# Choosing PSUM accumulation banks by the planner's count of when they come free, instead of from one ring

## The chip, the core and the metric

The kernel runs on one core of a Trainium2 chip. The time is device microseconds for one launch, the median of several launches. The engines are called as the profile calls them: PE (TensorE, matmul), DVE (VectorE), ACT (ScalarE), POOL (GpSimd) and SP (SyncE, which issues most of the DMAs here). PE writes its results into PSUM, which the kernel uses as eight banks of 128 x 512 float32. Only DVE and ACT read the banks in this kernel, and a bank can take a new result when its last reader is through.

## What is computed

The output mixes two branches over the same input `x` (2048 tokens of 576 channels) with a gate for each token:

```python
g = sigmoid((x * gate_w).sum(-1, keepdims=True))
a = ssm_branch(x, A_re, A_im, B_re, B_im, C_re, C_im, log_dt, Dskip)
b = expert_branch(x, w_q, k1, k2, u, v)
return g * a + (1 - g) * b
```

The first branch builds, for each channel, a kernel of 2048 taps from 128 complex exponentials, convolves `x` with it by FFT, and adds `x * Dskip`. The second has 32 heads. Each head forms a query of 2 x 128 for a token, scores each half against 64 keys, takes the best two of each half, combines them to four candidates and keeps two. That makes 64 experts of 4096 for each token, with softmax weights `g`:

```python
act = gelu(einsum("nd,nhkd->nhk", x, u[top_e]))
out = einsum("nhk,nhk,nhkd->nd", g, act, v[top_e])
```

## The kernel before

The kernel doesn't gather experts. It multiplies `x` with all of `u`, selects by one-hot matrices, and multiplies the selected weights with all of `v`. Its matmuls, with the names that they bear in the profile:

- `a` (128 tiles of 14 matmuls of 128 x 512, named `a{c}_{tb}_{j}`): `x` times `u` for one eighth `c` of the experts, one quarter `tb` of the tokens and one 128-row piece `j`. `act_post` copies each tile out of its bank as `go` (ACT or DVE) and stores it in `g_d`.
- `s` (128 tiles of 14 matmuls, `s{c}_{t}`): the scores of token tile `t` (of 16) in column group `c` (of 8). `scores_top` reads the bank sixteen times on DVE: eight MAX8, then eight FIND_INDEX8.
- `wb`, `wn`, `sq`, `x`, `kn`: folding of query weights with keys (giving `whl`), and norms for scaling.
- `kP`, `wbp`, `kb`: phases and taps of the convolution kernel, 36 channel groups `c` (`k_front`, `k_gen`, `k_store`); `gn` is a norm for them. ACT, POOL and DVE work on each group between its `kP` and its `kb`.
- `u` (`u1_{p}`, 16 steps that need four banks at once), `k` (`k1_{w}`), `pr`/`pi`, `pv`: FFT of the input, FFT of the taps, products of the spectra and the step back (`u_stage1`, `k_stage1`, `products`). `k_stage1` starts when all `kb` are stored.
- `tr`: transposes of the indices, after the gating of all column groups.
- `S{t}_{q}_{hb}`: for token tile `t` and quarter `q`, two banks of 16 short matmuls of one-hot matrices `A` and `Bg`, which DVE builds. DVE multiplies them into `gl`, and `split` makes `wh` of `gl` by an ACT and a DVE pass. Token tiles come in the order 0, 15, 1, 14, 2, ...
- `o` (16 token tiles of two banks, 3,072 matmuls of 128 x 288): `wh` times `vhl`, which `v_work` makes of `v` in eight pieces `vhl0` to `vhl7`, each by ACT and by DVE or POOL passes. `y` (8 steps that need four banks at once) is the last step of the inverse FFT, added into `ya`.

**What sets the order.** The Python program carries its own planner. Each piece of work is a generator, `clock` is the planner's time on PE, and each engine has a count of when it will be free (`Engine.free`). `rdy` holds when a tile will be ready. A generator yields until its inputs are ready and then writes its instructions at the end of the engines' queues. The main loop (lines 1719 to 1757) chooses between an `s` tile and an `a` tile. It holds `s` back when DVE's count is far ahead of PE (`lag`), and `pump` lets the other generators in between groups of three matmuls. On the chip each engine runs its queue strictly in that order, so an instruction that waits holds up all behind it.

**Banks.** A quota by tag says how many banks the three kinds of users may hold: `sc` (the `s`, `a` and `o` tiles), `kb` (convolution work) and later `wb` (the same after line 921). Each tag has a list of times at which its own places come free (`slots`). `need(tag, n)` waits until `n` places of that tag are free by the planner's clock, `take` removes the earliest, and `free(tag, outs)` adds one with the time at which the reader's output will be ready. Which of the eight banks a tile gets is not in that count: the pool is asked for a buffer of one shared tag.

```python
288  quota(sc=4, wb=0, kb=4, hw=1, slot=9, go=3, m8=2, raw=1, ko=1)
290  def bank(tag, name):
291      take(tag, name)
292      t = ps.tile([128, 512], F32, tag="ps", name=name, bufs=8)
1696 bank_free = lambda: slots["sc"] and min(slots["sc"]) <= clock[0]
```

A matmul into a bank whose former readers have not finished waits on PE, whatever the quota said.

Of the kernel before, what the change touches and what calls it, by code (L numbers as in the profile page):

```python
# [138 lines left out]
def body(ctx: ExitStack, tc: tile.TileContext, xT, au, par, logdt, dskip, gatew, wq, kT, uT, vv,  # L139
# [5 lines left out]
    clock = [0.0]  # L145
# [296 lines left out]
    def squares(a, r, sq, dst):  # L442

        acc = newcol(), newcol()
        S.activation(sq[:, 0:4, :], a, AF.Square, accum_out=sc[:, acc[0]])
        S.activation(sq[:, 4, :], r, AF.Square, accum_out=sc[:, acc[1]])
        yield from ready(sq)
        tag = side()
        yield from need(tag)
        p = bank(tag, "sq")  # L450
        mm(p[:, 0:2], onesb, short(acc[0].start, 2), True, True, 0.05)
        yield from ready(p)
        V.tensor_reduce(out=dst, in_=p[:, 0:2], axis=AX, op=OP.add)
        free(tag, dst)
# [5 lines left out]
    def x_norm(tb, sq):  # L460

        yield from need("kb")
        p = bank("kb", f"x{tb}")
        if tb == 0:
            for k in range(8):
                mm(p, onesb, sq[:, k % 4, :], True, True)
            while not marks["s"]:
                yield 0.1
        for k in range(5):
            mm(p, onesb, sq[:, k, :], k == 0, k == 4)  # L470
        normed.append(tb)
# [4 lines left out]
        free("kb", nx)  # L476
# [23 lines left out]
    def scale_first(a, r, sq, keep=None):  # L500
# [16 lines left out]
        free("kb", out[0])  # L517
# [80 lines left out]
    def w_half(c, h, w):  # L598
# [22 lines left out]
        free(tag, s)  # L621
# [19 lines left out]
    def w_tail(c, k, pb, hl, rem, o, count, s, tag):  # L641
        yield from ready(pb, s)
        if k < 4:
            yield from split(hl[:, 0, k:k + 2, o], hl[:, 1, k:k + 2, o], pb.rearrange("p (k n) -> p k n", k=2), s)
            free(tag, hl)
        else:
# [8 lines left out]
            free(tag, rem)  # L655
# [29 lines left out]
    def k_params():  # L685
# [82 lines left out]
        for h in range(2):  # L768
# [5 lines left out]
            free("kb", sc[:, b[h]])  # L774
# [10 lines left out]
    def k_factors(g):  # L785
# [8 lines left out]
        free("kb", t)  # L794
# [6 lines left out]
    def k_front(c):  # L801
# [18 lines left out]
        def reduce(z, p):  # L820
# [9 lines left out]
            free("kb", CS)  # L830
# [82 lines left out]
    def k_store(c, kb):  # L913
# [9 lines left out]
        free("kb", ko)  # L923
# [28 lines left out]
    def scores_top(c, t, pb):  # L952
# [14 lines left out]
        free("sc", i8)  # L967
# [76 lines left out]
    def turned(t, p):  # L1044
# [3 lines left out]
        free("wb", idxT)  # L1048
# [14 lines left out]
    def u_stage1():  # L1063
# [18 lines left out]
        def tail(p, tag, pbs):  # L1082
            for g in range(2):
                o = us[:, 2 + g, :]
                for hh in range(2):
# [4 lines left out]
                    free(tag, ov)  # L1090
# [43 lines left out]
    def k_stage1(ksb, fk, tabs):  # L1134
        enter, leave, count = ring(3)

        def tail(w, o, pbs):
            yield from ready(*pbs)
            for hh in range(2):
                copy(o[:, 288 * hh:288 * hh + 288], pbs[hh][:, :288])  # L1140
                free("wb", o)
# [22 lines left out]
    def products(ff):  # L1164
# [21 lines left out]
        def tail(g, pbs, v):  # L1186

            t = ff.tile([128, 2, 2, PW], F32, tag="tt", name=f"tt{g}", bufs=2)
            for n, p in enumerate(pbs):
                yield from ready(p)  # L1190
                copy(t[:, n].rearrange("p u q -> p (u q)"), p)
                free("wb", t)
# [10 lines left out]
        def store(g, pvs):  # L1203
# [4 lines left out]
            for n in range(2):  # L1208
                free("wb", vos[k])
# [167 lines left out]
    def act_post(c, tb, j, pb):  # L1377
# [8 lines left out]
        free("sc", go)  # L1386
# [9 lines left out]
    def v_norm():  # L1396
# [12 lines left out]
        for b in range(48):  # L1409
# [22 lines left out]
            free(tag, sv[0])  # L1432
# [62 lines left out]
    def prep(t):  # L1495
# [14 lines left out]
        for q in range(4):  # L1510
# [13 lines left out]
            for hb, pS in enumerate(pbs):  # L1524
# [5 lines left out]
                free("wb", *gl)  # L1530
# [27 lines left out]
    def y_part():  # L1558
# [16 lines left out]
        for p in range(NT // 2):  # L1575
# [16 lines left out]
            for n, a in enumerate(ya):  # L1592
                yield from ready(a, *pbs[2 * n:2 * n + 2])
                for hh in range(2):
                    ah = a[:, 288 * hh:288 * hh + 288]
                    V.scalar_tensor_tensor(ah, pbs[2 * n + hh][:, :288], iuk, ah, op0=OP.mult, op1=OP.add)
                    free("wb", a)
# [12 lines left out]
    def half_rows(t, a, po, hh):  # L1610
        cs = slice(288 * hh, 288 * hh + 288)
        V.scalar_tensor_tensor(a[:, cs], po[hh][:, :288], om[:, t:t + 1], a[:, cs], op0=OP.mult, op1=OP.add)
        free("sc", a)
# [44 lines left out]
    def k_split():  # L1658
# [10 lines left out]
        free("kb", kk)  # L1669
# [26 lines left out]
    bank_free = lambda: slots["sc"] and min(slots["sc"]) <= clock[0]  # L1696
# [143 lines left out]
```

## Time and profile before

| | us |
|---|---|
| median of 3 runs (lowest, highest) | 1455.22 (1452.94, 1456.87) |
| the profiled execution's own time | 1458.63 |
| span of its trace, first to last instruction | 1456.8 |
| mean granted TensorE clock | 0.998 |
| PE busy | 1430.8 (98%) |
| DVE busy | 1221.0 (84%) |
| ACT busy | 776.0 (53%) |
| POOL busy | 521.4 (36%) |

The span is the time between the first and the last instruction; the run's own time has 1.8 us around it. Busy time is the share in which an engine had an instruction in work. In the list of waits, a row names the waiting engine and its tile, the engine and tile that ended the wait, and then the sum in us, the number of such waits and the longest. In the timeline a row has start, duration, engine, line, operation, output and input tiles and count, and in square brackets the idle time before it with what ended that. PEclk is the granted TensorE clock as a share of full speed.

### The profile page before, as it was taken

The page shows a single profiled execution, that of the slowest core. Times are in us where ns is not written, and L with a number is a line of the kernel's source. Part 1 is how long each engine was busy: PE and PEld are TensorE (multiplying, and loading weights), DVE is VectorE, ACT ScalarE, POOL GpSimd, SP SyncE. Part 2 cuts the span into 40 slices and gives each one's busy share as a digit, 9 for nine tenths or more (in the row PEclk, how much of TensorE's full clock was granted, in tenths as well). Part 3 has the DMA queues.
Part 4 walks back from the last instruction along what each step waited for, and adds up shares of the span by engine and source line. Part 5 has one row for each costly group of instructions (what it writes and reads, how often), then busy time and mean ns, then how long its engine had stood idle before and what let it go on. Part 6 is the DMA issues. An engine that isn't in the chain of part 4 may idle for free.

```text
span 1456.8 us, 36814 instructions
## 1 busy us (share of the span) xinstructions
PE 1430.8 (98%) x14103; PEld 853.9 (59%) x14105; DVE 1221.0 (84%) x4569; ACT 776.0 (53%) x1304; POOL 521.4 (36%) x510
## 2 busy tenths in 40 slices
PE   7999999999999999999999999999899999999998
PEld 3445445555454445455555444447687887888787
DVE  6898889889877996885989898689998988998860
ACT  6346776796685776834556564576333224323310
POOL 0335357536446446210237999623000100110100
PEclk9999999999999999999999999999999999999999
DMA  8235223442434432269486776787343432342400
GB/s 306 77 112 172 88 80 109 126 138 72 129 106 124 116 104 92 62 211 292 157 304 216 266 250 214 255 265 228 130 122 110 140 120 98 125 148 67 157 9 17
DMA packets 134352, 215.44 MB, mean 148 GB/s; under 512 B 10912, under 2 KB 79904, under 8 KB 127776
## 3 DMA queue, kind: packets, MB, share of 16 engines
q1 hardware_dynamic: 134080, 213.01, 45.3%
q8 instruction: 111, 1.82, 0.5%
q14 instruction: 65, 0.53, 0.1%
q10 hardware_dynamic: 96, 0.07, 0.0%
HBM read 141.74 MB, written 71.30 MB: 146 GB/s over the span
## 4 chain that ended last, share of the span: by engine, by line
PE 85%; DVE 5%; DMA 2%; ACT 1%; issue 0%; POOL 0%; SPq 0%; DVEq 0%; POOLq 0%
PE o L214 25%; PE s L214 22%; PE a L214 22%; PE S L214 4%; PE kb L214 2%; PE wb L214 2%; PE pr L214 2%; DMA vn<-in_au_dram 1%; PE y L214 1%; PE kP L214 1%; PE k L214 1%; DVE i L134 1%; PE pv L214 1%; PE u L214 1%; DVE vhl L134 1%; DVE m L134 1%
## 5 line engine op out<-in xcount | busy, mean ns | idle before, releaser
L214 PE MATMUL o<-vhl,wh 128*128 128x288 f16 x3072 | 389.2, 287 | 0.0
L214 PE MATMUL s<-whl,xb 128*128 128x512 f16 x1536 | 365.0, 379 | 0.0
L214 PE MATMUL a<-xb,uhl 128*128 128x512 f16 x1536 | 359.5, 379 | 0.2 <-DVE go L134 0.2
L214 PEld LDWEIGHTS <-wh 128*128 128x128 f16 x3072 | 296.8, 98 | 77.5 <-issue 3.7
L214 PEld LDWEIGHTS <-xb 128*128 128x128 f16 x1792 | 170.6, 98 | 208.5 <-issue 14.3
L214 PEld LDWEIGHTS <-uhl 128*128 128x128 f16 x1536 | 147.1, 98 | 176.3 <-issue 3.2
L134 DVE FIND_INDEX8 i<-m,s 128x8 uint32<-128x64 f32 x1024 | 206.9, 226 | 0.0
L134 ACT ACTIVATE wh<-gl,s_wg 128x1024 f16<-128x1024 f32 x64 | 69.0, 1137 | 203.6 <-DVE gl L134 203.6
L134 DVE MAX8 m<-s 128x8 f32<-128x64 f32 x1024 | 146.4, 217 | 27.1 <-PE s L214 26.6
L134 POOL TENSOR_TENSOR CS<-CS,ex 128x512 f32<-128x512 f32 x72 | 97.9, 1389 | 147.6 <-DVE ex L134 146.2
L134 POOL TENSOR_TENSOR ya<-ya,db 128x576 f32<-128x576 f32 x16 | 31.8, 1995 | 320.3 <-DVE Bg L134 159.2
L134 ACT ACTIVATE go<-a,i_a 128x512 f32<-128x512 f32 x92 | 61.5, 682 | 89.1 <-PE a L214 63.9
L134 DVE TENSOR_TENSOR gl<-S,gl 128x256 f32<-128x256 f32 x256 | 90.3, 416 | 13.5 <-PE S L214 10.1
L134 POOL TENSOR_TENSOR e<-aN,rt 128x512 f32<-128x512 f32 x72 | 83.1, 1174 | 49.9 <-PE kb L214 43.8
L134 DVE SCALAR_TENSOR_TENSOR wh<-gl,s_wg,wh 128x1024 f16<-128x1024 f32 x64 | 91.1, 1455 | 11.3 <-ACT wh L134 11.3
L134 DVE TENSOR_TENSOR Bg<-Be,vals 128x1024 f16<-128x1024 f16 x128 | 91.7, 758 | 2.2
L134 ACT ACTIVATE gl<-gl 128x1024 f32<-128x1024 f32 x64 | 63.4, 1044 | 34.1 <-DMA gl<-g_d 34.1
L214 PE MATMUL S<-Bg,A 128*128 128x64 f16 x2048 | 73.6, 194 | 6.4 <-DVE Bg L134 6.4
L214 PEld LDWEIGHTS <-A 128*128 128x128 f16 x2048 | 71.4, 98 | 11.4 <-DVE Bg L134 4.9
L134 DVE TENSOR_TENSOR A<-iota_a,vals 128x2048 f16<-128x2048 f16 x64 | 77.9, 1218 | 0.0
L134 DVE MATCH_VALUE_LOAD i<-m,s 128x8 f32 x1024 | 76.3, 75 | 0.1
L214 PE MATMUL s<-wrem,xb 128*128 128x512 f16 x256 | 76.2, 379 | 0.0
(206 smaller groups left out, 2156.6 us busy)
## 6 DMA issues: line engine op xcount, KB each, us to landing
g_d<-go SPq DMA_DIRECT2D x128, 256.0 KB, 2.4
gl<-g_d SPq DMA_DIRECT2D x32, 1024.0 KB, 5.5
wq<-in_wq_dram SPq DMA_DIRECT2D x16, 1152.0 KB, 5.6
su_d<-us SPq DMA_DIRECT2D x32, 288.0 KB, 2.6
sk_d<-k1o SPq DMA_DIRECT2D x32, 288.0 KB, 3.7
vn<-in_vv_dram SPq DMA_DIRECT2D x32, 288.0 KB, 4.1
ui<-su_d SPq DMA_DIRECT2D x16, 576.0 KB, 4.0
ki<-sk_d SPq DMA_DIRECT2D x16, 576.0 KB, 5.5
```

The costliest lines, as they stand in the source:

```text
L134: return f(*a, **k)
L214: T.matmul(o, l, r, start=start, stop=stop)
```

## The change

The eight banks become eight pool tags of one buffer each, `ps0` to `ps7`. A list `vacant` holds for each bank that nobody owns the time at which it will come free, and `held` counts how many each tag owns. `need` asks that the quota has room and that the `n` earliest of all vacant banks are free by the planner's clock; it looks again after 0.2 to 0.3. `bank` takes the earliest vacant one of all, whichever tag had it before. `free(tag, outs, of=tile)` gives back the quota at once and puts the bank on the list with its time. Every call of `free` for a bank gets `of=`; the other uses of `quota`, `need`, `take` and `free` stay.

```diff
+    banksets = "sc", "kb", "wb"
+    held = dict.fromkeys(banksets, 0)
+    vacant = [(0.0, n) for n in range(8)]
+    number = {}
     def quota(**kw):
         for tag, n in kw.items():
+            if tag in banksets:
+                caps[tag] = n
+                continue
...
     def need(tag, n=1):
+        while tag in banksets:
+            lst = sorted(vacant)
+            if held[tag] + n <= caps[tag] and len(lst) >= n and lst[n - 1][0] <= clock[0]:
+                return
+            yield max(0.2, min(0.3, lst[n - 1][0] - clock[0])) if len(lst) >= n else 0.3
...
-    def free(tag, *outs):
+    def free(tag, *outs, of=None):
+        if of is not None:
+            held[tag] -= 1
+            vacant.append((max([clock[0]] + [rdy.get(key(x), 0.0) for x in outs]), number[of.tensor.name]))
+            return
...
     def bank(tag, name):
-        take(tag, name)
-        t = ps.tile([128, 512], F32, tag="ps", name=name, bufs=8)
+        held[tag] += 1
+        b = min(vacant)
+        vacant.remove(b)
+        t = ps.tile([128, 512], F32, tag=f"ps{b[1]}", name=name, bufs=1)
+        number[t.tensor.name] = b[1]
...
-        free("sc", i8)
+        free("sc", i8, of=pb)
...
-    bank_free = lambda: slots["sc"] and min(slots["sc"]) <= clock[0]
+    bank_free = lambda: held["sc"] < caps["sc"] and vacant and min(vacant)[0] <= clock[0]
```

Since the planner decides by these times, the order on every engine moves too, though no instruction of PE, and almost none of the others, is added or taken away (some copies go from ACT to DVE or back). Three places follow; the first number in a name is the piece or token tile, and a last long number only counts tiles.

PE, where the spectra's products begin (`pr0`, in `products`), before:

```order
L214 MATMUL s6_3_9777<-whl6_8521,xb0_148 128x512
L214 LDWEIGHTS onesb_71
L214 MATMUL wn7_0_9800<-sc_75,onesb_71 128x1
L214 MATMUL pr0_9803<-ui0_9659,cst_70 64x256 x2
L214 MATMUL pi0_9804<-ui0_9659,cst_70 64x256 x2
L214 MATMUL pr0_9803<-ki0_9660,cst_70 64x256 x2
L214 MATMUL pi0_9804<-ki0_9660,cst_70 64x256 x2
```

The same place of the change:

```order
L214 LDWEIGHTS xb3_577
L214 MATMUL s4_14_8766<-whl4_7345,xb3_577 128x512
L214 MATMUL pr0_8802<-ui0_8710,cst_70 64x256 x2
L214 MATMUL pi0_8803<-ui0_8710,cst_70 64x256 x2
L214 MATMUL pr0_8802<-ki0_8711,cst_70 64x256 x2
L214 MATMUL pi0_8803<-ki0_8711,cst_70 64x256 x2
```

The products now stand behind score tile 14 of column group 4 instead of tile 3 of column group 6: the convolution branch comes earlier by some 20 score tiles, and score tiles come later.

DVE, from the passes that make `wh` of token tile 15 to the first quarter of token tile 1, before:

```order
L134 SCALAR_TENSOR_TENSOR wh15_1_13434<-gl15_0_13021,s_wg_92,wh15_0_13433 128x1024
L134 SCALAR_TENSOR_TENSOR vhl6_12950<-vhl7_12951,sci_76,vhl6_12950 128x576
L134 SCALAR_TENSOR_TENSOR wh15_1_13434<-gl15_1_13022,s_wg_92,wh15_0_13433 128x1024
L134 SCALAR_TENSOR_TENSOR vhl7_12951<-vs_13332,sci_76,vhl7_12951 128x576
L134 SCALAR_TENSOR_TENSOR ya0_13355<-y0_0_0_13574,iuk_94,ya0_13355 128x288
L134 SCALAR_TENSOR_TENSOR ya0_13355<-y0_0_1_13579,iuk_94,ya0_13355 128x288
L134 SCALAR_TENSOR_TENSOR ya15_13360<-y0_1_0_13584,iuk_94,ya15_13360 128x288
L134 SCALAR_TENSOR_TENSOR ya15_13360<-y0_1_1_13589,iuk_94,ya15_13360 128x288
L134 TENSOR_TENSOR gl1_0_13436<-S1_0_0_13618,gl1_0_13436 128x32x8
```

The same place of the change, from the second half of the one-hot matrices on:

```order
L134 TENSOR_TENSOR Bg1_1_13410<-Be1_1_13408,vals_80 128x1024 x2
L134 SCALAR_TENSOR_TENSOR wh15_1_13385<-gl15_0_13068,s_wg_92,wh15_0_13384 128x1024
L134 TENSOR_TENSOR iwv_93<-sci_76 128x1
L134 TENSOR_SCALAR om_82<-gA_81 128x16
L134 SCALAR_TENSOR_TENSOR wh15_1_13385<-gl15_1_13069,s_wg_92,wh15_0_13384 128x1024 x2
L134 TENSOR_TENSOR gl1_0_13395<-S1_0_0_13523,gl1_0_13395 128x32x8
```

The passes for `vhl6` and `vhl7` and those for `ya` no longer stand between token tile 15 and token tile 1: the `vhl` passes come before the first one-hot matrix of token tile 0 (one of them just behind it), the `ya` passes after the third quarter of token tile 1.

PE, two successive `a` tiles in the change:

```order
L214 MATMUL a4_1_3_5567<-xb1_149,uhl4_3977 128x512
L214 LDWEIGHTS wrem0_114
L214 MATMUL a4_1_3_5567<-xb1_149,wrem0_114 128x512
L214 LDWEIGHTS uhl4_3977
L214 MATMUL a4_2_0_5609<-xb2_515,uhl4_3977 128x512
```

The two `a` tiles stand one behind the other in both programs; in the change they have the same bank, so nothing stands between the last matmul of the one and the first of the other while the bank is read.

More of the change, by code (lines that the diff above doesn't have):

```diff
@@ L475, in x_norm @@
         V.tensor_reduce(out=nx[:, tb:tb + 1], in_=p, axis=AX, op=OP.max)
[L476 removed]
+        free("kb", nx, of=p)
     def x_first():
@@ L516, in scale_first @@
             V.tensor_copy(keep, p[:, 0:1])
-        free("kb", out[0])
+        free("kb", out[0], of=p)
         return out
@@ L620, in w_half @@
         V.tensor_copy(invW[:, 2 * c + h:2 * c + h + 1], i)
-        free(tag, s)
+        free(tag, s, of=p)
         while c not in halves:
@@ L793, in k_factors @@
         copy(t.rearrange("p k n -> p (k n)"), p[:6 * CH])
-        free("kb", t)
+        free("kb", t, of=p)
         par_t[g] = t
@@ L829, in reduce @@
                 V.tensor_sub(v[:, 2 + z], v[:, z], pv)
-            free("kb", CS)
+            free("kb", CS, of=p)
             left[0] -= 1
@@ L922, in k_store @@
         V.tensor_sub(kz[:, 1], kq, kz[:, 0])
-        free("kb", ko)
+        free("kb", ko, of=kb)
         yield from ready(ko)
```

30 lines of the change are left out of this document (15 added, 15 removed).

## The prediction

> **What bounds the kernel now.** I read the page's first part, then the list of what PE waited for, then windows and timelines at those waits.
>
> ```profile
> span 1456.8 us, 36814 instructions
> ...
> PE 1430.8 (98%) x14103; PEld 853.9 (59%) x14105; DVE 1221.0 (84%) x4569; ACT 776.0 (53%) x1304; POOL 521.4 (36%) x510
> ...
> PE 85%; DVE 5%; DMA 2%; ACT 1%; issue 0%; POOL 0%; SPq 0%; DVEq 0%; POOLq 0%
> ```
>
> PE is busy for all but 26.0 us, and 85% of the chain that ended last is PE's own work. The change adds no matmul and takes none away. So it can only win what PE idles, and what PE does slowly because it idled. It can lose without such a limit. The waits on PE, all of them:
>
> ```profile
> PE sq L214 <- ACT xb L134: 9.1, 3, 5.0
> PE S L214 <- DVE Bg L134: 6.4, 4, 4.6
> PE u L214 <- DVE uh L134: 1.9, 2, 1.4
> PE kb L214 <- issue: 1.6, 1, 1.6
> PE pi L214 <- DVE i L134: 1.3, 1, 1.3
> PE sq L214 <- ACT uhl L134: 1.1, 1, 1.1
> PE pv L214 <- DVE m L134: 0.4, 1, 0.4
> PE pi L214 <- DVE m L134: 0.2, 1, 0.2
> PE a L214 <- DVE go L134: 0.2, 1, 0.2
> ```
>
> The 9.1 us are the first loads, where the order of the change is the same for the first 20 us of PE's work. Waits for a bank are those in which the instruction that ended the wait only read another tile's bank: `pi` and `pv` for score readers, `a` for `go`. They sum to 1.3 + 0.4 + 0.2 + 0.2 = 2.1 us. The longest one:
>
> ```profile
> 859.61 0.23 DVE L134 FIND_INDEX8 i<-m,s 128x8 uint32<-128x64 f32 x1
> ...
> 859.99 0.43 PE L214 MATMUL pi<-ui,cst 64*64 64x256 f32 x2 [1.31 <-DVE i L134]
> ```
>
> `pi` needs nothing of the scores. It stands there until DVE's last FIND_INDEX8 of a score tile has ended, at 859.84. That is the ring at work: the bank given was not the free one. But such places are rare.
>
> **The wait that is worth more is not a bank's.**
>
> ```profile
> 1027.94 0.23 PE L214 MATMUL S<-Bg,A 128*128 128x64 f16 x1 [4.57 <-DVE Bg L134]
> 1028.53 1.81 PE L214 MATMUL S<-Bg,A 128*128 128x64 f16 x31 [0.36 <-DVE Bg L134]
> ...
> 1020.00:1025.00 5.00, 3.36 (x28) 2.45 (x25) 5.00 (x7) 1.38 (x2) 2.62 (x2) 1.00 0.99 283
> 1025.00:1030.00 5.00, 1.70 (x30) 1.59 (x31) 4.97 (x11) 0.00 (x0) 0.00 (x0) 0.76 0.90 376
> 1030.00:1035.00 5.00, 5.00 (x30) 3.23 (x28) 4.96 (x10) 0.00 (x0) 0.00 (x0) 0.55 0.02 7
> ```
>
> The window rows give length, busy time of PE, PEld, DVE, ACT and POOL, PEclk, DMA share and GB/s. PE loses 4.57 + 0.36 = 4.93 us to the third quarter of token tile 1, while DVE has no gap. Then the granted clock falls: (1 - 0.76) x 5 + (1 - 0.55) x 5 = 3.45 us more. Together 8.4 us. [...]
>
> Why DVE was late, from the end of token tile 0's first two quarters to that wait:
>
> ```profile
> L134 DVE TENSOR_TENSOR Bg<-Be,vals 128x1024 f16<-128x1024 f16 x19 | 18.8, 1029 | 0.3
> ...
> L134 DVE SCALAR_TENSOR_TENSOR wh<-gl,s_wg,wh 128x1024 f16<-128x1024 f32 x8 | 13.2, 1674 | 0.0
> ...
> L134 DVE SCALAR_TENSOR_TENSOR vhl<-vhl,sci,vhl 128x576 f16<-128x576 f32 x11 | 9.1, 845 | 0.8 <-issue 0.8
> ...
> L134 DVE SCALAR_TENSOR_TENSOR vhl<-vs,sci,vhl 128x576 f16<-128x576 f32 x3 | 4.7, 1577 | 0.0
> L134 DVE SCALAR_TENSOR_TENSOR ya<-y,iuk,ya 128x288 f32<-128x288 f32 x4 | 1.9, 504 | 0.0
> L134 DVE TENSOR_SCALAR go<-a,i_a 128x512 f32<-128x512 f32 x1 | 0.7, 742 | 0.0
> ```
>
> These are groups of DVE between 949.3 and 1028.5. Fourteen `vhl` passes, 13.8 us, sit among the one-hot matrices for which PE waits.
>
> **The change part by part.** The bank's name and the lists are Python at build time: no instruction, no cost. What acts is the choice of bank and the new order.
>
> *Term 1, the old bank waits: -2.1 us.* Between -2.1 and 0: they go if DVE's count in the planner is true there, and stay if DVE runs later than counted.
>
> *Term 2, the wait at token tile 1: -8.4 us.* In the new order 13 of those 14 `vhl` passes come before the stretch, 11 x 0.845 + 2 x 1.577 = 12.4 us. The four `ya` passes come after it (1.9), one `wh` leaves (1.7), two more `go` enter (1.5). DVE has 12.4 + 1.9 + 1.7 - 1.5 = 14.5 us less to do. PE too comes sooner, so I count what stands between the first `S` of token tile 0 and that third quarter, before and now: 151 and 162 `a` matmuls, 186 and 108 `o`, 320 and 320 `S`, 16 and no `y`. Their prices, from the chain of waits:
>
> ```profile
> 969.72 16.84 PE a L214 x78
> ...
> 998.67 13.23 PE o L214 x108
> ...
> 1011.90 2.08 PE y L214 x32
> ...
> 1036.10 0.97 PE S L214 x32
> ```
>
> They are 0.216 for an `a`, 0.1225 for an `o`, 0.0303 for an `S`, 0.13 for a `y` (two records each). That makes 67.2 us before and 57.9 us now: PE comes 9.3 us sooner, DVE 14.5 us, a gain of 5.2 us on a wait of 4.93. It is narrow. But with POOL's own share of `vhl` earlier too, `Bg` should come down from its 1,029 ns. A remaining wait of 1 or 2 us would not bring back the fall of the clock: the waits of 1.3 to 1.6 us above had none. I take the whole 8.4; the bounds are 0 and 8.4. The `vhl` passes meet `a` tiles that PE can run meanwhile: at token tile 0's first `S` the change has 162 `a` matmuls left, 35 us; without that cover the 12.4 us would lie on PE's path.
>
> *Term 3, new bank waits: +4.0 us.* The quota is now given back when the reader is written, so `sc` can take banks that only `kb` held before, and all eight turn round faster. I count reuses in which PE's work between the old owner's last matmul and the new one's first is shorter than such a tile's readers took at the median of before: 11 before, 21 now. Before, they cost 2.1 us, 0.19 each. At that price 21 cost 4.0. The lower bound is the one place with nothing between, `a4_1_3` and `a4_2_0`:
>
> ```profile
> L214 PE MATMUL a<-xb,uhl 128*128 128x512 f16 x1536 | 359.5, 379 | 0.2 <-DVE go L134 0.2
> ...
> L134 ACT ACTIVATE go<-a,i_a 128x512 f32<-128x512 f32 x92 | 61.5, 682 | 89.1 <-PE a L214 63.9
> ```
>
> The last matmul's result is out 379 ns after its start, the copy takes 682, and the next matmul would have started after 216: at least 0.85 us. Behind it in PE's queue stand the score tiles, and DVE, which works off older ones, waits for none of them soon. The upper bound is ten more waits as long as the longest before, 2.1 + 10 x 1.3 = 15 us.
>
> *Moved at no cost.* The convolution branch comes some 20 score tiles earlier on all engines and on SP's queue. PE's sum stays, since score tiles fill what `kb` and products leave, as now; without them it would be the price of the waiting itself, rival two. From token tile 2 on the order on PE is the same but for a few rows.
>
> *Sum.* The profiled execution took 1458.63 with 1456.8 in the span, 3.4 over the median of the runs. Its terms, -2.1 - 8.4 + 4.0 = -6.5, would bring it to 1452.1; from the median, 1455.2 - 6.5 = **1448.7 us**.
>
> **The rivals.** *One: the waits only change places.* PE waits when DVE is later than the planner counts, whatever bank is chosen, and a new wait of 5 us with its 3.45 us of slow clock elsewhere takes back term 2: 1455.2 - 2.1 + 4.0 - 8.4 + 8.4 = 1457, or with the old bank waits gone and no new ones, 1453. For it: the margin at token tile 1 is 0.3 us. That the change doesn't do what it says belongs here: it trusts the planner's clock, not the chip's. Against: outside that stretch PE met no wait over 1.6 us in all of 100 to 940 us.
>
> *Two, slower: DVE becomes the bound where products meet scores.*
>
> ```profile
> 620.00:940.00 320.00, 318.06 (x2982) 162.13 (x2972) 264.17 (x1600) 171.94 (x464) 180.27 (x243) 1.00 0.71 238
> ...
> L134 DVE TENSOR_TENSOR Bg<-Be,vals x128: 678/691/1896, 942.8 to 1396.9; 128x1024 f16<-128x1024 f16 x128
> ```
>
> Between tile 4 of column group 4 and tile 8 of group 5 the change has 84 us of PE's work against 81 us of DVE's, by the mean times of their groups; before, DVE had 83% of PE's 318 us over this whole phase. `Bg` (minimum, median, maximum) shows that an operation of DVE can take 2.7 times its usual time. Lengthened by 20%, DVE needs 97.6 us, 13.6 more than PE. Some 4 us are kept by banks, so 9.6 us and 3.45 us of clock: 1448.7 + 13 = 1462. It decides from about 8% on. Against: at 81 of 84 the means already hold such lengthening. [...]
>
> *Three: the other middle waits fall too* (`u` 1.9, `kb` 1.6, `sq` 1.1, the rest of `S` 1.5) and no new ones come: 1455.2 - 2.1 - 8.4 - 6.1 + 4.0 = 1443 with term 3 kept. Nothing in the order speaks for all of it.
>
> **How the numbers follow.** Forecast 0.55, rival one 0.20, two 0.18, three 0.07. The forecast's own range is 1445 (term 3 at 0.85) to 1452 (a rest of term 2). The range over all is 1444 to 1461: it leaves out most of rival three and the upper half of two. What a measurement of this kernel can tell from no change is 0.3%, 4.4 us, so faster is below 1450.9 and slower above 1459.6. Faster: rival three and nearly all of the forecast, 0.59. Same: the forecast's upper end and most of rival one, 0.19. Slower: rival two and the worst of one, 0.22.
>
> **What would show it.** Term 1: no `pi` or `pv` row that waits for DVE `i` or `m`. Term 2: PE's row `S` from DVE `Bg` falls from 6.4 to under 3 us, and PEclk stays at 1.00 after 1000 us. Term 3: rows of `a`, `kP`, `u` or `s` that wait for `go`, `CS`, `us` or `i`, 4 us in all, one at about 440 us. Rival two would show PE's busy share falling between 600 and 800 us with DVE full. I am wrong if PE's idle time comes out above 26 us, or if the saving is there with the wait at token tile 1 unchanged.

## The result, and the profile after

The change made the kernel slower: 1466.0 us in the median of 6 runs (1464.4 to 1467.3) beside 1456.6 for the kernel before (6 runs, 1452.9 to 1459.2). The ratio is 1.0066, with a 95% interval of 1.0051 to 1.0081, so 7 to 12 us were lost where 6.5 were forecast as gained. The profiled execution took 1465.7.

The first part of the page of the changed kernel:

```profile
span 1463.1 us, 36804 instructions
...
PE 1432.3 (98%) x14105; PEld 852.2 (58%) x14105; DVE 1214.8 (83%) x4575; ACT 768.0 (52%) x1294; POOL 529.1 (36%) x518
```

The span grew by 6.3 us. PE's idle time went from 26.0 to 30.8 us and its busy time from 1430.8 to 1432.3. DVE and ACT have less to do than before (by 6 and 8 us), so no engine became the bound by its sum. The list of what PE waited for, in the same kernel (us in total, times, longest):

```profile
PE sq L214 <- ACT xb L134: 8.7, 3, 5.0
PE a L214 <- DVE ko L134: 3.9, 1, 3.9
PE sq L214 <- ACT uhl L134: 2.8, 1, 2.8
PE a L214 <- DVE sc L134: 2.7, 1, 2.7
PE S L214 <- DVE Bg L134: 1.7, 2, 1.3
PE a L214 <- DVE i L134: 1.5, 2, 1.3
PE a L214 <- ACT go L134: 1.5, 3, 0.8
PE S L214 <- DVE gl L134: 1.4, 1, 1.4
PE s L214 <- DVE wrem L134: 1.3, 1, 1.3
PE pv L214 <- DVE i L134: 0.4, 1, 0.4
```

The wait for `Bg` fell from 6.4 to 1.7 us, and the `u` and `kb` rows of before (1.9 and 1.6) are gone. But rows in which PE waits for the reader of another tile's bank now sum to 12.9 us (`ko`, `sc`, `i` twice, `go` with one of 0.2 us, `gl`, `wrem`), where they were 2.1. The two largest are in the first half, where the convolution's kernel is built. Here is the timeline at the largest, the matmuls of `a3_3_3` at 365.46:

```profile
359.69 2.07 DVE L134 TENSOR_TENSOR Y<-e,CS 128x1024 f32<-128x1024 f32 x1
...
360.64 3.48 POOL L134 TENSOR_TENSOR ex<-ex,gN 128x512 f32<-128x512 f32 x2
361.45 0.10 PEld L214 LDWEIGHTS <-uhl 128*128 128x128 f16 x1
361.86 1.35 DVE L134 TENSOR_TENSOR e<-e,CS 128x512 f32<-128x512 f32 x1
...
363.13 1.53 DVE L134 SCALAR_TENSOR_TENSOR e<-e,CS 128x512 f32<-128x512 f32 x1
...
364.73 0.68 DVE L134 TENSOR_TENSOR ko<-kb,ko 128x512 f16<-128x512 f32 x1
365.33 0.20 DVE L134 TENSOR_SCALAR sc<-wn,kk 128x1 f32<-128x1 f32 x1
...
365.46 1.01 PE L214 MATMUL a<-xb,uhl 128*128 128x512 f16 x2 [3.94 <-DVE ko L134]
```

The weights of the `a` tile were loaded at 361.45. Its inputs had long been there. It stands until DVE has read the bank of `kb16`, and DVE comes to that only after three long passes and two short copies on other tiles. With the trace's rows put to the tiles of the program, all eight banks at 361.6 us were these (start of the last matmul, end of the last read, in us):

```
tile      last matmul   last read by DVE ends
kb16         356.3        365.4   (the bank that a3_3_3 took)
wn2_1        358.4        365.5
kP20_1       356.7        366.8
kP21_0       358.5        367.3
kP20_0       356.4        368.7
wb2_1_0      360.1        369.3
wb2_1_4      361.3        370.0
wb2_1_2      361.1        373.6
```

The source's count chose well: no bank came free earlier than the one it named. What is wrong is that there was nothing to choose from. All eight belong to the background (`kP`, `kb`, `wb`, `wn`, tag `kb` in the source, whose quota is four), all are computed, and all wait for one engine. At 495 us six banks of the background wait for DVE, the other two have been given to `wb3_1_0` and `wb3_1_2`, whose matmuls stand behind the `a` tile in PE's queue, and the wait is 2.68 us. These two and the 1.3 us for `wrem` (`s6_9` waits for the bank of `wb7_1_4`) are the waits for a bank of the background, 7.9 of the 12.9 us. The others, of 1.4 us at most each, are for banks of `a`, `s` or `S` tiles.

The clock followed. Windows of the changed kernel (length, busy time of PE, PEld, DVE, ACT and POOL, granted clock, DMA share, GB/s):

```profile
360.00:365.00 5.00, 1.52 (x53) 1.48 (x49) 4.90 (x6) 0.86 (x2) 4.23 (x4) 0.94 0.47 128
365.00:370.00 5.00, 4.54 (x11) 1.57 (x11) 4.84 (x13) 2.67 (x7) 5.00 (x4) 0.50 0.68 188
370.00:375.00 5.00, 5.00 (x29) 2.04 (x27) 2.95 (x3) 3.09 (x6) 3.87 (x4) 0.88 0.57 179
...
495.00:500.00 5.00, 3.65 (x25) 1.69 (x26) 4.90 (x12) 0.05 (x1) 4.23 (x5) 0.75 0.78 200
500.00:505.00 5.00, 5.00 (x138) 3.80 (x140) 3.17 (x5) 3.73 (x6) 4.72 (x4) 0.91 0.80 241
...
1025.00:1030.00 5.00, 5.00 (x68) 3.37 (x64) 4.96 (x6) 0.00 (x0) 2.76 (x2) 1.00 0.28 74
```

After the wait of 3.94 us the clock is missing (0.06 + 0.50 + 0.12) x 5 = 3.4 us, after that of 2.68 us (0.25 + 0.09) x 5 = 1.7 us. At token tile 1, where before lost 3.45 us in this way, it is at 1.00. So the clock's loss went from 3.4 to 5.1 us. A little of it falls in the waits themselves (the 0.94 is from before 365 us, where PE still waits): PE's busy time grew by 1.5 us, not by 1.7.

The account of the span: bank waits +10.8, the wait for `Bg` -4.7, clock +1.7, the `u` and `kb` rows -3.5, the `sq` rows +1.3, two small new rows +0.5. That makes +6.1 of the 6.3.

### The profile page after: what moved, and what is told of

Same layout as the page of the kernel before. It is cut to its first block, busy times and chain, and to the rows that moved or that the text cites. A ratio compares the mean times of both kernels' runs of the same rounds, so it can differ in the third digit from the quotient of the medians.

```text
span 1463.1 us, 36804 instructions
## 1 busy us (share of the span) xinstructions
PE 1432.3 (98%) x14105; PEld 852.2 (58%) x14105; DVE 1214.8 (83%) x4575; ACT 768.0 (52%) x1294; POOL 529.1 (36%) x518
## 4 chain that ended last, share of the span: by engine, by line
PE 89%; DVE 6%; DMA 2%; ACT 1%; issue 1%; POOL 0%; SPq 0%; DVEq 0%; ACTq 0%; POOLq 0%
PE o L214 25%; PE a L214 25%; PE s L214 23%; PE S L214 4%; PE kb L214 2%; PE pr L214 2%; PE wb L214 2%; DVE i L134 1%; PE y L214 1%; PE pv L214 1%; DVE m L134 1%; PE u L214 1%; PE kP L214 1%; DVE e L134 1%; PE k L214 1%
## 5 line engine op out<-in xcount | busy, mean ns | idle before, releaser
L134 DVE MAX8 m<-s 128x8 f32<-128x64 f32 x1024 | 145.6, 212 | 21.2 <-PE s L214 20.9
L134 ACT ACTIVATE go<-a,i_a 128x512 f32<-128x512 f32 x77 | 52.0, 684 | 91.1 <-PE a L214 60.1
L134 DVE SCALAR_TENSOR_TENSOR wh<-gl,s_wg,wh 128x1024 f16<-128x1024 f32 x63 | 86.7, 1406 | 13.7 <-ACT wh L134 13.7
L214 PE MATMUL a<-xb,wrem 128*128 128x512 f16 x256 | 76.0, 380 | 0.0
```

The costliest lines, as they stand in the source:

```text
L134: return f(*a, **k)
L214: T.matmul(o, l, r, start=start, stop=stop)
```

## The experiments

Eighteen kernels were run besides the two. The table has them all. "Bank waits" are PE's waits that end with the last reader of the bank that the waiting tile takes, between 100 and 600 us. The idle times are the window's length less PE's busy time in it. Ratios are to the kernel before in the same session. "Reader ends" means that a bank counts against its tag until its reader is through, as before the change; "reader written" is the change's rule.

| kernel | quota returns when | time us | ratio (95%) | bank waits 100-600 | PE idle 100-600 | PE idle 940-1100 |
|---|---|---|---|---|---|---|
| before | reader ends | 1456.6 | 1 | 0.0 | 3.1 | 6.4 |
| pick | reader ends | 1457.9 | 1.0006 (0.9995 to 1.0017) | 0.0 | 3.6 | 4.1 |
| both4 | reader ends | 1510.2 | 1.0368 (1.0354 to 1.0382) | 0.0 | 1.4 | 52.9 |
| sham_b | reader ends | 1509.8 | 1.0373 (1.0345 to 1.0402) | 1.6 | 4.2 | 30.6 |
| sham_b2 | reader ends | 1486.9 | 1.0209 (1.0189 to 1.0229) | 3.5 | 3.5 | 26.7 |
| the change | reader written | 1466.0 | 1.0066 (1.0051 to 1.0081) | 9.6 | 9.6 | 3.1 |
| admit | reader written | 1470.9 | 1.0090 (1.0076 to 1.0103) | 13.4 | 13.7 | 1.9 |
| cost | reader written | 1475.8 | 1.0127 (1.0110 to 1.0144) | 19.2 | 19.4 | 1.9 |
| margin | reader written | 1486.4 | 1.0200 (1.0185 to 1.0215) | 23.0 | 26.1 | 1.5 |
| sham_a | reader written | 1479.9 | 1.0159 (1.0139 to 1.0178) | 10.6 | 19.3 | 5.4 |
| sham_a2 | reader written | 1469.6 | 1.0086 (1.0066 to 1.0105) | 9.0 | 9.5 | 4.9 |
| score4 | background: written | 1472.0 | 1.0104 (1.0088 to 1.0119) | 11.1 | 12.1 | 1.9 |
| back4 | background: ends | 1476.4 | 1.0128 (1.0113 to 1.0144) | 0.3 | 7.3 | 4.4 |
| back5 | background at most 5 | 1452.6 | 0.9964 (0.9951 to 0.9977) | 0.0 | 2.9 | 4.6 |
| back6 | at most 6 | 1457.6 | 1.0013 (1.0004 to 1.0023) | 0.4 | 3.4 | 4.4 |
| back7 | at most 7 | 1459.8 | 1.0010 (0.9994 to 1.0026) | 5.4 | 5.4 | 2.9 |
| six_five | 6, then 5 | 1454.0 | 0.9973 (0.9959 to 0.9987) | 0.4 | 3.8 | 3.7 |
| six_ring | 6, then 5; ring | 1462.1 | 1.0037 (1.0023 to 1.0050) | 5.6 | 7.0 | 3.8 |
| six_sham | at most 6 | 1465.0 | 1.0051 (1.0035 to 1.0068) | 3.1 | 9.9 | 3.0 |
| six_sham2 | at most 6 | 1471.3 | 1.0094 (1.0075 to 1.0113) | 0.3 | 4.4 | 10.2 |

### The choice of bank and the admission, apart

The change has two parts: which bank a tile takes, and when it may take one. The first run has only the former. Its order of instructions is that of before on every engine:

```diff
     def free(tag, *outs, of=None):
+        if of is not None:
+            vacant.append((max([clock[0]] + [rdy.get(key(x), 0.0) for x in outs]), number[of.tensor.name]))
         if owed[tag]:
...
     def bank(tag, name):
         take(tag, name)
-        t = ps.tile([128, 512], F32, tag="ps", name=name, bufs=8)
+        b = min(vacant)
+        vacant.remove(b)
+        t = ps.tile([128, 512], F32, tag=f"ps{b[1]}", name=name, bufs=1)
```

> The rule for admitting work as before (each reader's quota, the same order of instructions on every engine), but the bank given is the one that the count says comes free first, under a name of its own. Theory 'order' (the change lost its time because the new admission moves work so that all eight banks are in use and their readers run behind the count): this is as fast as before or gains what the ring lost, 1453 to 1457 us beside 1456.6, and waits of PE for a bank come to 2 us or less. Theory 'choice' (the bank that the count names is often the wrong one): 1460 us or more, with PE waiting 6 us or more for banks, and S<-Bg still near 6 us, since the order is that of before.

The second has the change's admission, and so its order on every engine, and takes banks from the ring:

```diff
-        t = ps.tile([128, 512], F32, tag=f"ps{b[1]}", name=name, bufs=1)
+        t = ps.tile([128, 512], F32, tag="ps", name=name, bufs=8)
```

> The change's admission (the same order of instructions as the change on every engine), but banks from the old ring of eight. Theory 'order': no faster than the change, 1466 us or above, with bank waits of PE of 12 us or more, some of them at other tiles, since the ring adds its own misses to the late readers. Theory 'choice': the gain at token tile 1 stays (S<-Bg under 3 us) and the new bank waits go, so about 1456.6 - 5 to 1456.6, bank waits under 4 us.

The choice alone changed nothing that can be told from noise (1.0006; its 1457.9 us are 0.9 above the range that 'order' gave), and the new order with the old ring was slower than the change by 0.0024 of the time, 3.5 us, with an error of about 0.0020 (both intervals together). PE's waits in the second one, against 3.9 and 2.7 in the change:

```profile
PE a L214 <- DVE ko L134: 8.4, 3, 3.9
PE a L214 <- ACT us L134: 2.8, 2, 1.6
```

So the loss comes with the new admission and its order, and the choice of bank makes it smaller. "Choice" is out.

### The planner's count

Two runs let the planner think worse of DVE or of banks. The first raises what it counts for a wide DVE operation beside a busy POOL:

```diff
-            wait = (0.55 if n >= 512 and len(aps) > 1 else 0.3) if G.free > max(V.free, clock[0]) else 0.0
+            wait = (0.9 if n >= 512 and len(aps) > 1 else 0.3) if G.free > max(V.free, clock[0]) else 0.0
```

> The change, with the planner's count for a DVE operation of two inputs of 512 elements or more while POOL is busy raised by 0.35 us (0.55 to 0.9), so that it counts about 2.04 for the Y pass that took 2.07, and 1.5 for the e pass that took 1.35 to 1.53. Theory 'count' (the waits are there because the planner believes banks free before DVE has read them): the 3.9 and 2.7 us waits of the k phase go, bank waits under 6 us in all, 1455 to 1461 us. Theory 'order' without it: another order with waits as long at other places, bank waits of 9 us or more and 1463 to 1470 us.

The second holds every bank for vacant 1 us later than counted:

```diff
-            vacant.append((max([clock[0]] + ...
+            vacant.append((1.0 + max([clock[0]] + ...
```

> The change, with every bank held to be vacant 1.0 us later than its reader's counted end, in the admission and in the choice. Theory 'count': tight reuses disappear, bank waits under 5 us, PE's idle time back to 26 us or less, 1453 to 1460 us. Theory 'order' without it: the waits are 2.7 to 3.9 us where they matter and a margin of 1.0 takes off no more than 1 us at each; 1462 to 1468 us. If fewer vacant banks starve PE of work to issue, idle time that no bank ends appears and it is slower than the change.

Both were slower still (1475.8 and 1486.4, beyond the ranges of either theory), with bank waits in the first half twice as long as the change's. "Count" had foretold that they go. My reading, which no run tests by itself, is that a count that lets banks come free later leaves fewer of them and does not hold the background back. The `Y` pass of the timeline above did run long, though; the group of all of them in the changed kernel (minimum, median and maximum):

```profile
L134 DVE TENSOR_TENSOR Y<-e,CS x36: 1197/1218/2067, 149.9 to 563.7; 128x1024 f32<-128x1024 f32 x36
```

2.07 against a median of 1.22: that is 0.85 of the 3.94 us, a part and not the whole.

### Whose banks they are

If the background fills the banks, a limit on it must take the waits away, and a limit on the other side must not. The edit, against the change:

```diff
+    ends = {t: [] for t in banksets}
+    used = lambda tag: held[tag] + sum(t > clock[0] for t in ends[tag])
+    most = lambda tag: 8 if tag == "sc" else caps[tag]
...
-            if held[tag] + n <= caps[tag] and len(lst) >= n and lst[n - 1][0] <= clock[0]:
+            if held[tag] + n <= caps[tag] and used(tag) + n <= most(tag) and len(lst) >= n and lst[n - 1][0] <= clock[0]:
...
+            ends[tag].append(max([clock[0]] + [rdy.get(key(x), 0.0) for x in outs]))
...
-    bank_free = lambda: held["sc"] < caps["sc"] and vacant and min(vacant)[0] <= clock[0]
+    bank_free = lambda: held["sc"] < caps["sc"] and used("sc") < most("sc") and vacant and min(vacant)[0] <= clock[0]
```

> The change, with one more condition for the background (the convolution, the weights, the products: tags kb and wb): it may have no more banks than its quota in use, counting those whose readers are written but not yet through. Activations and scores (tag sc) go on as in the change. Theory 'crowding' (with the quota given back when the reader is written, the background fills up to eight banks, four being computed and four queued at DVE, and PE's filler, the a and s tiles, finds none): the a waits for ko, sc and wrem of over 1 us go, bank waits under 4 us, 1450 to 1459 us. Theory 'denser' (the loss comes from the convolution coming earlier, so that DVE and POOL have more to do at once, whoever holds the banks): 1462 us or more, waits of the same length for DVE in the k phase. Theory 'borrowing' (the a and s tiles take banks of the background): 1462 us or more, with kP, kb, u or k tiles waiting.

The other three have another `most`: `caps[tag] if tag == "sc" else 8`, then `caps[tag]`, then `8 if tag == "sc" else caps[tag] + 2`.

> The other half: the a and s tiles may have no more than four banks in use, readers counted; the background goes on as in the change. 'Crowding': as slow as the change or slower, 1464 to 1478 us, with a and s tiles waiting 10 us or more for banks that kb, wn, u or kP tiles held. 'Borrowing': near before, 1453 to 1459 us. 'Denser': about the change, 1464 to 1468 us, so this run alone does not tell it from crowding.

> Both limits at once: no side has more than its quota in use, readers counted, as before; what stays of the change is that a bank's vacancy is looked up over all eight and the earliest is taken. 'Crowding': near before, 1453 to 1459 us, bank waits of PE under 4 us. 'Denser' does not apply, since the convolution should come about when it came before; it expects the same. A result of 1462 us or more would say that the quota is not what the change lost by.

> As the first, with six banks for the background instead of four: two that are queued at DVE beside four being computed, and two that only a and s tiles can have. 'Crowding' as a matter of degree: between the first run and the change, 1455 to 1464 us, bank waits of 4 to 10 us; if only the last two banks matter, as fast as the first run. 'Denser': 1464 us or more, since the convolution comes nearly as early as in the change.

The second came out in time as crowding said, at 1472.0 us; the `a` tiles' waits for the background's banks are 8.0 us where 10 were expected. The row that leads its list of bank waits:

```profile
PE a L214 <- DVE sc L134: 8.0, 2, 4.0
```

Each is an `a` tile that waits 4 us for the bank of a `wn`. "Borrowing" is out. The first and the last have 0.3 and 0.4 us of bank waits in the first half where the change has 9.6 (for the last I had given 4 to 10). The last, with the convolution's final `kP` at 550 us, 41 us earlier than before and 17 later than the change, is within 0.13% of before. So "denser" is out too: the work may come early, if it doesn't hold all the banks.

But crowding had said 1450 to 1459 for the first and 1453 to 1459 for both limits, and there it missed by far, though the bank waits are gone in both (0.3 and 0.0). For both limits I had written that 1462 us or more would speak against the quota as the reason; by that sign, 1510.2 us does, as far as times go. The lists of the first:

```profile
PE wn L214 <- ACT wj L134: 9.0, 3, 7.3
PE kb L214 <- issue: 5.8, 2, 3.6
PE S L214 <- DVE Bg L134: 5.1, 6, 2.3
```

and of the one with both limits:

```profile
PE S L214 <- DVE Bg L134: 46.7, 14, 13.7
```

With four banks the waits are elsewhere, and PE runs short of filler. In the first, 26 `a` tiles were left when the convolution's last `kP` ran, at 577 us; that is the number that the loop keeps back (`len(acts) > 26`), and the wait of 7.3 us for `wn` comes at 604 us. In the one with both limits no `a` tile was left at the first `S` of token tile 0, where before had 10 and the change 11, and PE waits for the one-hot matrices with nothing else to do. So the limit has a price at its other end. That a rule so near to that of before could lose 54 us raised another question: what does a new order cost by itself?

### The chance of an order

Two kernels count each ACT operation 0.010 us longer or shorter in the planner, with the rule of before; two do the same to the change:

```diff
-        t = 0.085 + 0.00083 * size(out)
+        t = 0.095 + 0.00083 * size(out)
```

> The kernel before, with one number of its planner changed that has nothing to do with banks: each ACT operation is counted 0.010 us longer (0.085 to 0.095). The order of the instructions comes out another from 45 us on, the rule for banks is untouched. Theory 'quota' (the change lost by giving the quota back early): about as before, 1453 to 1460 us. Rival 'any new order' (the constants of this kernel fit one order, and whatever makes another one loses some us by chance): 1460 to 1475 us, with waits of PE of 2 us or more that were not there before.

> As the one before it, but counted 0.010 us shorter (0.075). 'Quota': 1453 to 1460 us. 'Any new order': 1460 to 1475 us, and not the same time as its twin.

> The change with the same alteration (ACT counted 0.010 us longer): another order under the change's rule for banks. 'Quota': as the change or slower, 1463 to 1475 us, and a tiles wait again for banks of kb, wn, kP or u tiles, at other places. 'Any new order': anything from 1455 to 1475 us, and no clear distance to the altered kernels before.

> The change with ACT counted 0.010 us shorter. The same expectations as for its twin: 'quota' 1463 to 1475 us with a tiles waiting for the background's banks; 'any new order' 1455 to 1475 us.

A hundredth of a microsecond in the count, and the kernel before is 54 and 30 us slower. "Quota" as put there is out for the time: both altered orders cost the kernel before more than the change did. The other theory put its limit at 1475 us, and three of the four are above it. Yet the two rules lose in different places, and each in the same place every time. Under the rule of before the stretch from 100 to 600 us keeps PE fed, and most of the loss is at the one-hot stage. The stretches of 100 to 600, 600 to 940 and 940 to 1100 us in the first of the two with the rule of before:

```profile
100.00:600.00 500.00, 495.82 (x4757) 246.71 (x4756) 414.46 (x1737) 350.22 (x514) 252.52 (x210) 1.00 0.36 110
600.00:940.00 340.00, 331.87 (x2951) 167.69 (x2953) 287.98 (x1772) 179.41 (x444) 157.49 (x218) 0.98 0.61 209
940.00:1100.00 160.00, 129.44 (x1330) 80.20 (x1323) 137.09 (x208) 88.07 (x149) 59.73 (x49) 0.88 0.61 197
```

and the first and the last of these in its twin under the change's rule:

```profile
100.00:600.00 500.00, 480.72 (x4864) 239.01 (x4863) 426.47 (x1511) 359.16 (x524) 276.92 (x221) 0.98 0.38 117
...
940.00:1100.00 160.00, 154.57 (x1568) 102.22 (x1566) 130.49 (x217) 73.88 (x101) 24.21 (x16) 0.99 0.55 175
```

Over three orders each, the bank waits in the first half are 0.0, 1.6 and 3.5 us against 9.6, 10.6 and 9.0, and PE's idle time from 940 to 1100 us is 6.4, 30.6 and 26.7 against 3.1, 5.4 and 4.9. In both altered pairs the change's rule is the faster one, by 30 and 17 us. The kernel before is an order that happens to have little of either loss, or was picked for it.

Not all that the twin idles in the first stretch is a bank's. Of its 19.3 us, 10.6 are; `wn` waits 7.8 us more there for ACT's `wj`:

```profile
PE wn L214 <- ACT wj L134: 8.7, 3, 6.6
PE kP L214 <- DVE nu L134: 7.6, 1, 7.6
```

The 7.6 us are those of a `kP`, a tile of the background itself, for the bank of a score tile. When this wait begins, six banks are the background's and two hold score tiles; at the longest wait of the other altered order (6.8 us, an `a` tile) it is seven and one `a` tile.

**What the planner's own clock says.** Building the program gives `clock` at the last matmul, without a run. It is 1456.6 us for before and 1465.0 for the change (measured 1456.6 and 1466.0), 1495.6 and 1480.6 for the altered orders of before (1509.8 and 1486.9), 1478.0 and 1463.7 for those of the change (1479.9 and 1469.6). Between 100 and 600 us of that clock PE stands still for 21.2 us in the change's plan and for 4.2 in that of before; 2.7 of the 21.2 are just ahead of `a3_3_3` and 3.3 just ahead of `a5_0_1`, the two tiles that waited 3.9 and 2.7 us on the chip. So the plan already has the sign of the change. It also has these two waits, because by its own count no bank is vacant earlier; that speaks against "count" more directly than the two runs above. The plan is not exact: over the twenty kernels it is off by up to 18 us.

### The limit under that chance, and its steps

Six banks for the background with the altered counts, then seven banks, then six for tag `kb` and five for `wb` (`most` is `caps[tag] + 2` and `caps[tag] + 1`):

> Six banks at most for the background, as in the run that came out near before, with ACT counted 0.010 us longer (the alteration that took the kernel before to 1510 us and the change to 1480). Theory 'crowding' (a limit below eight takes away the a and s tiles' waits in the first 600 us in any order): PE waits under 4 us in sum between 100 and 600 us, and the time is below the change's twin, 1455 to 1472 us. Rival 'chance of one order' (six was lucky once): 1475 to 1510 us, or waits of 8 us and more between 100 and 600 us.

> The same with ACT counted 0.010 us shorter (twins: before's rule 1487, the change's 1470). 'Crowding': under 4 us of waits between 100 and 600 us and 1452 to 1468 us. 'Chance of one order': 1470 us or more, or 8 us of waits and more in that stretch.

> Seven banks at most for the background, nothing else altered. 'Crowding': between six (1457.6) and the change (1466), with the a and s tiles' waits between 100 and 600 us between the two as well, 1458 to 1466 us. 'Chance of one order': no relation, 1450 to 1490 us.

> Six banks at most for the convolution and the weights of the first half (tag kb), five for those after it (tag wb): the candidate to beat both kernels. 'Crowding': no bank wait of over 1 us before 600 us, and as PE then idles some 3 us less than with six for both, 1450 to 1456 us. 'Chance of one order': 1460 us or more.

In the altered orders the limit holds the bank waits at 3.1 and 0.3 us, against 10.6 and 9.0 without it. The first one's other idle time there is not a bank's:

```profile
PE kb L214 <- issue: 6.8, 2, 4.1
PE a L214 <- ACT go L134: 2.2, 3, 0.8
```

By the letter of the expectation (waits of any kind under 4 us there) both miss, with 9.9 and 4.4, and each meets one sign of the rival (8 us of waits or more; 1470 us or more). In time the first kept within it (1465.0, 15 us below its twin without the limit) and the second did not (1471.3 against at most 1468): it met 10.2 us of idle time at the one-hot stage, and is no faster than its twin (1.0094 against 1.0086). So the limit's effect on the waits is seen in both orders, that on the time in one. With seven the bank waits are 5.4 us, between 0.4 and 9.6, but the time is that of six (1.0010 and 1.0013). The fourth beats before: 0.9973, interval 0.9959 to 0.9987.

### The ring once more, and five banks

> The order of the version with six and five banks (1454.0), but the banks from the ring of eight: what the choice of bank is worth in an order whose banks aren't all in use. Beside it stand the two pairs measured: no difference in the order of before (1457.9 with the choice, 1457.1 with the ring), 4.9 us in the crowded order of the change (1466.0 and 1470.9). Theory 'the choice pays only where all eight banks are in use': within 2.5 us of 1454.0, bank waits of PE at most 2.5 us above. Rival 'the choice pays in any order but that of before, to which the ring was fitted': 1457 us or more, bank waits of 4 us and more.

The edit is that of the second run. The order is the one of six and five banks, but the ring costs 1.0037 / 0.9973, 0.64% or 9 us (error about 3):

```profile
PE a L214 <- DVE ko L134: 2.8, 2, 1.6
...
PE kP L214 <- DVE ko L134: 1.9, 1, 1.9
```

My theory, that the choice pays only where all banks are in use, fell: it was worth nothing in the order of before, 3.5 us in the crowded one, and 9 here. Why the order of before alone does well with the ring is not shown; that it was picked with the ring in place would explain it.

> Five banks at most for the background all the way, the last step of the row four (1476.4), six (1457.6), seven (1459.8), eight (1466.0). 'Crowding' says that the a and s tiles' bank waits in the first 600 us are gone at five, as they are at four and six: under 2 us. What four lost (9.0 us at wn, 5.8 at kb) should come back in part, since the background is held up: 1454 to 1468 us. 'Chance of one order': no relation, 1450 to 1490 us.

1452.6 us, below the range that I gave and the fastest of all, 0.36% below before (interval 0.23 to 0.49). Its whole list:

```profile
PE sq L214 <- ACT xb L134: 9.2, 3, 5.3
PE kb L214 <- issue: 2.9, 1, 2.9
PE S L214 <- DVE Bg L134: 2.5, 3, 1.7
PE y L214 <- DMA gl<-g_d: 2.0, 1, 2.0
PE wn L214 <- ACT wj L134: 0.7, 1, 0.7
PE s L214 <- ACT tt L134: 0.2, 1, 0.2
PE a L214 <- DVE go L134: 0.2, 1, 0.2
```

Bank waits are 0.4 us in all. The row of limits four to eight reads 1476, 1453, 1458, 1460, 1466 us: crowding on one side, and on the other what a limit of four costs. Given the 3 to 54 us that the altered counts moved the time by, a step of 5 us in this row says little by itself; the bank waits (0.3, 0.0, 0.4, 5.4, 9.6) carry the reading.

## Why the prediction was wrong

**Term 1 (-2.1) was right in kind.** The `pi` rows are gone; 0.4 of `pv` and 0.2 of `a` stayed: -1.5.

**Term 2 (-8.4) was right.** `S` from `Bg` fell by 4.7 us, to 1.7 where under 3 was foretold, and the 3.4 us of clock there came back: -8.1. The margin had been put at 0.3 us, so that so little of the wait was left is in part luck.

**Term 3 (+4.0) is the step that failed, by its size.** The mechanism was named (the quota is given back when the reader is written, so that banks of one tag are taken by another), and so was the place at about 440 us, where 0.8 us is lost. But I counted tight reuses and priced each at 0.19 us, the mean of waits for a single late reader under the old quota. The new waits measured 12.3 us, and the two longest took the clock with them for another 5.1: 17.4 where 4.0 stood. The upper bound of 15 held for the waits alone, but it had no clock in it. A count of reuses doesn't see what decided here: whether the eight banks are all on DVE's queue at one time. Then the wait is what is left of that queue when PE arrives. The reads in the table above end 7 to 13 us after the last matmuls began. I had looked at it from the wrong side as well: I wrote of scores that take banks of the convolution, and at the two longest waits it was the convolution and the weights that held those of PE's filler.

**"Moved at no cost"** rested on the same filler: "score tiles fill what `kb` and products leave". They do, if they are given a bank.

With what I hadn't foreseen (`u` and `kb` -3.5, `sq` and others +1.8) the measured terms sum to -1.5 - 8.1 + 17.4 - 1.7 = +6.1.

**The rivals.** Rival one, that the waits only change places, has the nearest mechanism, down to the slow clock behind a new wait; it allowed for one such place, and there were two, and some smaller ones; its 1457 us is 9 too low. Rival two did not happen: where it put the loss, from 600 to 800 us, PE is busy for 198.7 of 200 us. The rows:

```profile
600.00:700.00 100.00, 99.85 (x868) 55.27 (x867) 84.36 (x577) 59.22 (x159) 33.52 (x72) 1.00 0.77 263
700.00:800.00 100.00, 98.88 (x1010) 49.44 (x1008) 88.25 (x558) 60.99 (x162) 71.49 (x85) 1.00 0.73 246
```

The lengthening of DVE operations, with which it reckoned, is there in the first half, beside a busy POOL: of the 36 `Y` passes of the changed kernel, the 26 with POOL busy for less than 30% of their time took 1.23 us at most, while of the other ten four took 1.22 to 1.23 and six 1.87 to 2.07. Of the kernel before's 18 `Bg` passes that began between 950 and 1029 us, the seven with POOL idle took 0.69 us at most, and of the other eleven five took 1.65 to 1.89. At the largest new wait the lengthening was 0.85 of the 3.94 us, so it was not what decided. Rival three had no support.

**The test that I set** ("wrong if PE's idle time comes out above 26 us") was met, at 30.8. In this pair of kernels the sign was wrong through the new bank waits and the clock behind them: by the account above, without these 17.4 us the change would have gained. A limit of four to six banks on the background, with the rest of the change as it is, took the waits from 9.6 to 0.4 us or less, and in the two altered orders from 10.6 and 9.0 to 3.1 and 0.3. It is not shown that the change's rule is worse than that of before in general: in both altered pairs it is the faster one. What the chance of an order adds to a single pair of times isn't separated from this by the times, only by where PE waits.

## What to carry to other kernels

When one engine's reads free a shared set of buffers, limit what the work that feeds it may hold, counted until the reader is through; else that work can end up holding them all, and the filler that should cover for it gets none. Too low a limit has its own price (four banks here). Before pricing a new allocation rule by the reuses that are tight, ask which tiles hold all the buffers at the worst moment, and how long the queue is that they wait in. Where a planner writes the order, read its own end time and its own idle time first: here they had the sign. And alter a constant that has nothing to do with the change: if the time moves by more than the change does, judge the rule by where the waits are, over several orders, and not by one pair of times.

## What the runs showed of the hardware

In the traces of the kernel before and of the change, from 20 us to the last us of the span, PE's granted clock is 0.50 in three stretches and 1.00 elsewhere. In before it is 0.50 from 1027.6 to 1034.5 us, at the wait of 4.57 us; in the change from 364.4 to 371.2 us, at the wait of 3.94, and from 497.5 to 500.9 us, from 1.1 us after the end of the wait of 2.68. At half the clock these 6.8, 6.8 and 3.4 us cost 3.4, 3.4 and 1.7 us. PE's other waits of 1 us or more from 20 us on had no such stretch: four of 1.0 to 1.4 us and the stop of 1.6 us in before, four of 1.3 to 1.4 us in the change, and one of 2.8 us there (`sq` for `uhl`, 848.2 to 851.0 us). The prediction's price of 3.45 us is near what came with the two waits of 3.94 and 4.57 us, 3.4 us each. Of the waits of 2.68 and 2.80 us one came with a loss of 1.7 us more and the other with none; what decides between them is not shown.

Ten of the twenty kernels have one or two stops of PE at a `kb` tile's matmuls, the longest of 1.0 to 4.1 us, at which the profile shows nothing that PE waits for ("issue"). In before (454.3 to 455.9 us) and in the altered order above (302.7 to 306.8 us) `kb` matmuls run on both sides of it. Its length follows no edit (1.6 us in before, 2.9 in the fastest, 4.1 in the altered order above, none in the change). What it is was not tried.
